# A gated-attention and maxout kernel on one core: its hand-kept order table is replaced by another

## The chip, the cores and the metric

The kernel runs on one core of one Trainium2 chip. The metric is device time in microseconds of one execution, lower is better. Before the change three executions took 138.85, 139.35 and 139.71 us (median 139.35). The profiled execution is one more, of 139.14 us; the span that its profile covers is 137.4 us.

## The reference

Four batches, eight heads, 768 time steps, head size 48. A recurrent state per head is decayed by a gate and fed with an outer product; its readout, all heads side by side, goes through a two-branch maxout layer.

```python
f = 1.0 / (1.0 + np.exp(-f_logit))
for t in range(S):                                   # S = 768
    state = f[:, :, t, :, None] * state + np.einsum('bhd,bhe->bhde', k[:, :, t], v[:, :, t])
    y[:, :, t] = np.einsum('bhd,bhde->bhe', q[:, :, t], state)
x = y.transpose(0, 2, 1, 3).reshape(B * S, H * D)    # 3072 x 384
g = np.maximum(x @ w1, x @ w2)                       # d_ff = 1024
out = g @ w_out                                      # 3072 x 384
```

## The kernel before, in words

The 3072 rows are worked in twelve stages `s = 4 * w + b`: window `w` (0 to 2) of 256 rows of batch `b` (0 to 3). A window is two chunks of 64 row pairs. Inside a stage the recurrence is done in chunked form: logs of the gate are summed by a matmul, queries and keys are scaled by exponentials of the sums, and the readout is a masked product inside the chunk plus a product with the state carried in. The maxout is rewritten with `max(a, b) = b + relu(a - b)`, so the layer is `x @ (w2 @ w_out) + relu(x @ (w1 - w2)) @ w_out`; the product `m2 = w2 @ w_out` and the difference `wd = w1 - w2` are made on the core once.

One string, `ORDER`, fixes everything: the words are read from left to right and each issues one step, so each engine gets its instructions in the order of its words. A word is a step's letter, its stage or index, an engine (`a` ScalarE, `v` VectorE, `p` GpSimd, `s` the SyncE queue; in the traces ACT, DVE, POOL, SP) and after `@` a PSUM bank (0 to 7) or, for loads, one of 30 SBUF slots. Steps that the text speaks of:

- loads, all on the one SP queue: `Lf`, `Lq`, `Lk`, `Lv` (L124, a stage's gate logits, queries, keys, values, 384 KB each), `Wb` (L140, thirds of w2), `Wo` (L144, quarters of w_out), `Wa` (L137, quarters of w1);
- on ACT: `E` (L215) and `F` (L219), the gate's exponential and logarithm; `G`, `X`, `Z` (L223, L240, L245), further exponentials;
- on DVE or POOL: `e` (L226), `i` (L249), `j` (L253, DVE only), `K` and `Q` (L260, L263, the scaled keys and queries), `V` (a cast, L113), `N` (L401);
- on TensorE (PE): `C` (L230, L233) the sums, `t`, `u` the transposes of `K` and `Q` (L278 for stages 0 and 1, L285 after), `A` (L315) the chunk product, `D` (L379) the state's increment, `S` and `y` (L336) the readout, `wt` (L463) the transposes of w2, `wm` (L478) the product m2, `d` (L418, two of the eight column blocks of `x @ wd`), `o` and `p` (L440, output products), `h` (L492, matmuls of zeros into a bank that nobody reads);
- `U` copies the transposed chunks out of PSUM (L113, tile trs), `m` masks `A` (L321, DVE), `n` adds the state (L396, L398, DVE), `Y` copies the readout (tile xT), `r` is the relu out of PSUM (L427 on ACT, L429 on DVE), `ws` makes a quarter of `wd` (L488, DVE), `b` copies an output out of PSUM;
- `z` (tile look, L113) copies one column of the readout's banks after the first half of `S`; `y` writes these banks next and so waits for it.

In stages 9 to 11 `t`, `u` and `U` are replaced by transposing DMAs (`T`, L300). `gT`, which `r` writes and `o` reads, has two buffers, for even and for odd stages. An SP transfer waits for its slot to be free, and at most eight transfers are under way, since each takes one of eight completion semaphores in turn.

Of the kernel before, what the change touches and what calls it, by code (L numbers as in the profile page):

```python
# [21 lines left out]
Lq0s@10 Lv1s@14 Z0 u1@6 K1v U1.1a@6 X0 i0p Wb0s j0v t1@5 U1.0a@5 h3@7 A1.0@3 V1a A1.1@6 D1@0 Q0p wc0a Wb1s  # L22
Wb2s m1.0@3 K0p n1.0@2 Wo1s u0@5 wt0@0 Wo3s m1.1@6 wx0v@0 S1.0@3 wc1a z1v@3 wc2p t0@2 wt1@6 n1.1@0 U0.0a@2
g0p y1 g6p U0.1v@5 wo3p wo1a S1.1@3 wt2@0 wx1v@6 Y1.0v@3 wx2v@0 A0.0@6 Lv0s@27 Y1.1a@4 Wo2s A0.1@1 wo2a V0p
wm1@3 Wo0s Lf2s@20 E2 wm3@3 Wa3s m0.1@1 m0.0@6 D0@1 wm2@3 wo0p n0.0@0 S0.0@0 z0a@0 wm0@3 F2 g3p wn2a@5 y0
# [29 lines left out]
"""


ROOMS = (1, 13, 16, 22, 28, 21, 24, 11, 21, 26, 28, 18)
M2_LAST = (0,)
WHOLE = {0, 1}  # L60
ZEROS = 29
# [3 lines left out]
def kernel(  # L65
# [491 lines left out]
```

## Time and profile before

| what | value |
|---|---|
| median of three executions | 139.35 us |
| profiled execution / its span | 139.14 us / 137.4 us |
| PE busy | 124.0 us, 90% |
| DVE / ACT / POOL busy | 96.8 / 81.0 / 52.8 us |
| DMA, read and written | 23.59 MB and 4.72 MB; the queue took 87.6% of 16 engines' span |
| first real matmul | at 6.81 us |
| last matmul ends | at about 134.45 us |

Times in rows are microseconds from the span's start. In the timeline a row is start, duration, engine, line, operation, output and inputs with shapes, how many were merged, and in brackets the idle time of that engine just before it with what ended it. PEld is the loading of a matmul's weights, which lies beside the matmuls. In the windows' rows the share of each engine is busy us in that stretch.

### The profile page before, as it was taken

How to read it: one execution, taken by the hardware profiler on the slowest of the kernel's cores; microseconds unless marked ns; L12 is line 12 of the kernel's file. 1: busy time of each engine (PE TensorE's matmuls, PEld its weight loads, DVE VectorE, ACT ScalarE, POOL GpSimd, SP SyncE). 2: the span in 40 equal slices, each digit the busy share in tenths (PEclk: the TensorE clock that was granted, in tenths of full speed). 3: DMA queues.
4: the chain of work that ended last, by engine and by line, in shares of the span. 5: the costliest groups of instructions: out<-in, count | busy, mean ns of one | idle time of the engine just before them, and what ended most of it. 6: DMA issues, size and time to landing. Idle time of an engine off the chain costs nothing.

```text
span 137.4 us, 5529 instructions
## 1 busy us (share of the span) xinstructions
PE 124.0 (90%) x2451; PEld 91.0 (66%) x2451; DVE 96.8 (70%) x153; ACT 81.0 (59%) x129; POOL 52.8 (38%) x60
## 2 busy tenths in 40 slices
PE   1058999999999999999989899999999999999991
PEld 0034796677656888665877577667878768885570
DVE  6683869497998889998898974799782786400501
ACT  3687853579869688929788967543642311252320
POOL 6006754600028643567965108699391000000000
PEclk9999999999999999999999999999999999999998
DMA  3999999999999999999999999992699400800044
GB/s 97 271 261 303 404 348 329 337 295 237 253 272 260 239 268 245 238 260 242 269 265 249 265 266 307 261 131 49 239 154 297 193 5 0 338 10 5 0 199 145
DMA packets 60904, 30.24 MB, mean 220 GB/s; under 512 B 56656, under 2 KB 58576, under 8 KB 60880
## 3 DMA queue, kind: packets, MB, share of 16 engines
q1 hardware_dynamic: 60880, 29.89, 87.6%
q8 instruction: 19, 0.31, 1.1%
q14 instruction: 5, 0.04, 0.1%
HBM read 23.59 MB, written 4.72 MB: 206 GB/s over the span
## 4 chain that ended last, share of the span: by engine, by line
PE 45%; DMA 20%; DVE 16%; SPq 7%; issue 4%; ACT 3%; POOL 1%; DVEq 0%; POOLq 0%
PE banks L440 19%; PE banks L418 14%; DMA slots<-in_q_dram 9%; SPq L124 7%; PE banks L336 7%; DMA slots<-in_moe_w_out_dram 6%; DMA slots<-in_moe_w_dram 5%; DVE at_m L321 4%; PE banks L315 2%; DVE slots L253 2%; PE banks L285 1%; DVE qp L263 1%; DVE state L401 1%; PE banks L379 1%; POOL qp L263 1%
## 5 line engine op out<-in xcount | busy, mean ns | idle before, releaser
L440 PE MATMUL banks<-wo,gT 128*128 128x384 bf16 (+1 forms) x200 | 35.3, 320 | 0.0
L418 PE MATMUL banks<-xT,wd 128*128 128x256 bf16 x288 | 34.3, 273 | 1.0 <-DVE tmp_s L396 0.5
L418 PEld LDWEIGHTS <-wd 128*128 128x128 bf16 x288 | 27.1, 98 | 5.7 <-DVE wd L488 1.2
L321 DVE TENSOR_TENSOR at_m<-banks,mask 128x1024 bf16<-128x1024 f32 x24 | 28.9, 1217 | 2.7 <-PE banks L315 2.5
L440 PEld LDWEIGHTS <-gT 128*128 128x128 bf16 x200 | 19.2, 98 | 11.8
L427 ACT ACTIVATE gT<-banks 128x1024 bf16<-128x1024 f32 (+1 forms) x17 | 16.2, 971 | 11.1 <-PE banks L418 7.1
L429 DVE TENSOR_SCALAR gT<-banks 128x1024 bf16<-128x1024 f32 (+1 forms) x9 | 9.9, 1104 | 14.8 <-PE banks L418 6.9
L263 POOL TENSOR_TENSOR qp<-slots,dec 128x768 bf16<-128x768 f32 x7 | 13.6, 1947 | 12.6 <-ACT dec L245 6.7
L113 ACT COPY slots<-banks 128x384 f32<-128x384 f32 (+1 forms) x19 | 8.8, 461 | 13.9 <-PE banks L440 13.6
L440 PE MATMUL banks<-m,xT 128*128 128x384 bf16 (+1 forms) x75 | 15.8, 320 | 0.1
L113 ACT CAST xT<-banks 128x768 bf16<-128x768 f32 (+1 forms) x12 | 8.2, 692 | 9.6 <-PE banks L336 9.6
L215 ACT ACTIVATE gate<-slots 128x768 f32<-128x768 f32 x12 | 10.1, 843 | 6.3 <-DMA slots<-in_f_logit_dram 6.3
L113 POOL CAST vb<-slots 128x768 bf16<-128x768 f32 x8 | 6.7, 840 | 15.6 <-DMA slots<-in_v_dram 15.6
L336 PE MATMUL banks<-at_m,vb 64*64 64x128 bf16 x576 | 11.4, 225 | 0.3 <-ACT look L113 0.2
L260 POOL TENSOR_TENSOR kp<-slots,inv 128x768 bf16<-128x768 f32 x6 | 10.9, 1816 | 0.6 <-ACT inv L240 0.5
L336 PEld LDWEIGHTS <-vb 64*64 64x64 bf16 x576 | 9.8, 111 | 1.6 <-issue 1.6
L253 DVE SCALAR_TENSOR_TENSOR slots<-gate,slots 128x384 f32<-128x384 f32 x12 | 9.0, 752 | 2.1 <-DMA slots<-in_q_dram 2.1
L219 ACT ACTIVATE ell<-gate 128x768 f32<-128x768 f32 x12 | 10.1, 844 | 0.3
L315 PE MATMUL banks<-trs 48*64 48x128 bf16 x384 | 10.1, 227 | 0.0
L230 PE MATMUL banks<-e,u_inc 128*128 128x384 bf16 x12 | 4.2, 355 | 6.2 <-DVE e L226 6.2
L249 POOL TENSOR_TENSOR slots<-slots,one 128x384 f32<-128x384 f32 x5 | 5.6, 1112 | 11.0 <-DMA slots<-in_k_dram 11.0
L113 DVE COPY slots<-banks 128x384 f32<-128x384 f32 (+1 forms) x9 | 5.4, 596 | 5.9 <-DMA out_dram<-slots 4.7
(69 smaller groups left out, 178.3 us busy)
## 6 DMA issues: line engine op xcount, KB each, us to landing
slots<-in_f_logit_dram SPq DMA_DIRECT2D x12, 384.0 KB, 6.2
slots<-in_q_dram SPq DMA_DIRECT2D x12, 384.0 KB, 6.0
slots<-in_k_dram SPq DMA_DIRECT2D x12, 384.0 KB, 6.3
slots<-in_v_dram SPq DMA_DIRECT2D x12, 384.0 KB, 6.1
out_dram<-slots SPq DMA_DIRECT2D x11, 384.0 KB, 3.8
slots<-in_moe_w_dram SPq DMA_DIRECT2D x3, 512.0 KB, 6.0
slots<-in_moe_w_out_dram SPq DMA_DIRECT2D x4, 384.0 KB, 8.4
slots<-in_moe_w_dram SPq DMA_DIRECT2D x4, 384.0 KB, 7.4
```

Source lines behind the costliest of these rows:

```text
L113: (nc.scalar.copy if e == "a" else engines[e].tensor_copy)(out, in_)
L215: nc.scalar.activation(flat(gate[s]), flat(loaded[s]["f"]), AF.Exp, bias=0.0, scale=-1.0)
L219: nc.scalar.activation(flat(ell[s]), flat(gate[s]), AF.Ln, bias=1.0, scale=1.0)
L253: engines[e].scalar_tensor_tensor(out=even, in0=gate[s][:, :, 1, :], scalar=1.0, in1=even, op0=ALU.add, op1=ALU.mult)
L260: engines[e].tensor_mul(pad("kp", s)[:, :, :, 0:D], by_parity(loaded[s]["k"]), both(inv[s]))
L263: engines[e].tensor_mul(pad("qp", s)[:, :, :, 0:D], by_parity(loaded[s]["q"]), both(dec[s][:, 0:HD].rearrange("p (h d) -> p h d", h=H)))
L315: nc.tensor.matmul(out=ps[h * HC:(h + 1) * HC, j % 2, par, :], lhsT=chunk(s, 0, rows, j, h)[:, par, :], rhs=chunk(s, 1, rows, j, h), start ...
L321: nc.vector.tensor_mul(at[s][:, jj].rearrange("p r j a t -> p (r j) (a t)"), banks[:, b:b + 2, :].rearrange("p r (j x) -> p (r j) x", j=2) ...
L336: nc.tensor.matmul(out=ys[s][h][c * DP:(c + 1) * DP, blk // 2, :], lhsT=lhs[:, at_col + off:at_col + off + DP], rhs=rhs, start=(s, h, c) n ...
L418: nc.tensor.matmul(out=ps[:, f, :], lhsT=wd[:, fp, kt, f * C:(f + 1) * C], rhs=xT[g][:, kt, :], start=(kt == 0), stop=(kt == KT - 1))
L427: nc.scalar.activation(dst, src, AF.Relu)
L440: nc.tensor.matmul(out=ps, lhsT=lhs, rhs=rhs[:, out_cols], start=(i == 0), stop=(i == len(terms) - 1))
```

## The change

Only the table `ORDER` and the table `ROOMS` (the slots that outputs are staged in) differ. 568 words stand in both; the two `h` words (four matmuls of zeros in all) are gone. 70 words name another engine, most of the others another bank or slot, and nearly all stand elsewhere. Counted from the PE order, the tile shape of the matmuls (128x128, 64x128 or 64x64) changes 42 times in place of 51. GpSimd gives two `K`, two `Q`, two `V` and two `e` to other engines and takes three `i` and two `N` more; VectorE has, on balance, two `e`, two `K`, two `Q` and four `V` more and three `i`, two `N`, two `r` and two copies of w2's transposes fewer.

```diff
 ORDER = """
-g2v Lf1s@7 Lf0s@23 E1 F1 E0 e1v h1@3 g4p Lq1s@17 C1@7 F0 j1v Z1 e0v Q1v Lk1s@26 G1 C0@2 X1 i1v g7v G0 Lk0s@3
+Lf1s@11 E1 Lf0s@10 Lq1s@21 g2p F1 E0 Lk1s@24 e1v Wb1s Lv1s@25 g3v g0p F0 e0v j1v G0 C1@1 X1 Lk0s@3 Wb2s Z1
...
-ROOMS = (1, 13, 16, 22, 28, 21, 24, 11, 21, 26, 28, 18)
+ROOMS = (13, 20, 25, 26, 11, 16, 21, 0, 15, 25, 11, 2)
```

The SP queue, from the first load of values on, before. `in_moe_w_dram 128x1024` is w2 and `128x3x256` is w1; the `in_f_logit_dram` row is the gate of stage 2.

```order
L124 DMA slots<-in_v_dram 128x8x96
L140 DMA slots<-in_moe_w_dram 128x1024 x3
L144 DMA slots<-in_moe_w_out_dram 128x768 x2
L124 DMA slots<-in_v_dram 128x8x96
L144 DMA slots<-in_moe_w_out_dram 128x768 x2
L124 DMA slots<-in_f_logit_dram 128x8x96
L137 DMA slots<-in_moe_w_dram 128x3x256 x3
```

The same queue after, up to the same two weights.

```order
L124 DMA slots<-in_q_dram 128x8x96
L140 DMA slots<-in_moe_w_dram 128x1024
L137 DMA slots<-in_moe_w_dram 128x3x256 x2
L124 DMA slots<-in_v_dram 128x8x96
L144 DMA slots<-in_moe_w_out_dram 128x768 x3
L124 DMA slots<-in_f_logit_dram 128x8x96
L144 DMA slots<-in_moe_w_out_dram 128x768
```

Two quarters of w1 moved ahead of all of w_out, and one quarter of w_out behind the gate of stage 2, so that this gate is the 17th transfer where it was the 16th.

ACT around the gate of stage 2 (`gate_147`) and the look of stage 0, before:

```order
L113 CAST xT_403<-banks 128x6x64
L113 CAST wo<-slots 128x768
L215 ACTIVATE gate_147<-slots 128x768
L113 COPY look<-banks 128x1
L219 ACTIVATE ell_158<-gate_147 128x768
```

And after (`gate_148` is the gate of stage 2, `gT_481` the relu of stage 1):

```order
L113 COPY slots<-banks 128x8x128
L427 ACTIVATE gT_481<-banks 128x1024
L113 CAST wo<-slots 128x768
L215 ACTIVATE gate_148<-slots 128x768
L113 COPY look<-banks 128x1
L219 ACTIVATE ell_156<-gate_148 128x768
```

A relu of stage 1 now stands ahead; the look stays behind the gate's exponential in both.

PE at the program's start, as a piece of the difference (L492 are the matmuls of zeros):

```order
 L552 UNCONDITIONAL_BRANCH
-L492 LDWEIGHTS slots
-L492 MATMUL banks<-slots 128x512
 L230 LDWEIGHTS u_inc
 L230 MATMUL banks<-e_97,u_inc 128x384
```

The zeros ahead of the first sums are gone; so are the three that stood ahead of the first `A`.

More of the change, by code (lines that the diff above doesn't have):

```diff
@@ L20 @@
 ORDER = """
-g2v Lf1s@7 Lf0s@23 E1 F1 E0 e1v h1@3 g4p Lq1s@17 C1@7 F0 j1v Z1 e0v Q1v Lk1s@26 G1 C0@2 X1 i1v g7v G0 Lk0s@3
[L22 to L25, printed above, removed]
@@ new lines @@
+n1.0@2 wt1@5 wt2@0 S1.0@6 wc0a j0v g6v m1.1@2 K0p z1v@6 Q0p Wa2s ws2v wx1a@5 y1 S1.1@6 Wa3s u0@4 n1.1@2
+wx2v@0 ws3v Y1.0a@6 wt0@3 Lv0s@8 Wo1s Wo3s Wo2s Y1.1a@7 t0@7 d1.2@5 wo1p wo2p V0v U0.0v@7 d1.3@6 U0.1a@4
+wx0a@3 Lf2s@26 D0@1 A0.0@3 n0.0@0 S0.0@6 Wo0s wo0p n0.1@1 r1.1a@5 m0.0@3 wo3a E2 A0.1@5 wm1@0 m0.1@5 Lf3s@24
+Wa0s z0a@6 wm3@0 F2 e2v y0 S0.1@6 wm2@0 Y0.0v@6 G2 C2@3 Y0.1a@7 Wa1s E3 wm0@0 Lq3s@8 F3 Lq2s@2 ws0v e3v ws1v
+wn1a@1 wn2a@2 d0.2@4 d0.3@5 C3@2 Lk2s@22 j3v Z2 r0.1a@4 Lk3s@15 wn0v@0 Z3 N1.1p d0.0@6 Q3v d0.1@7 r0.0a@6
@@ new lines @@
+i7p m5.1@2 d4.2@0 Lq11s@15 r4.0a@6 G8 U6.2v@4 Q7p S5.0@6 r4.1a@0 z5v@6 A6.0@4 y5 m6.0@4 K7p E9 i8p D6@2
+A6.1@0 S5.1@6 n6.0@0 Lf10s@27 Y5.2a@6 o4.1@5 d5.3@2 m6.1@0 d5.0@0 Lv8s@12 V7a F9 N6.0v Lq9s@16 b4.1.0a@5 j8v
+d5.2@1 r5.1a@1 e9v S6.0@4 z6v@4 D7@6 S6.1@4 y6 n7.0@0 E10 Lv10s@17 C9@6 d5.1@1 Y6.2v@4 V8a r5.0a@0 Z9
+Lk10s@22 Lv9s@6 j9v Lk9s@28 o4.0@2 K8v Q8p X9 n6.1@2 F10 d6.3@1 N7.0p d6.2@0 b4.0.0v@2 n7.1@0 N5.1p G10
+Lf11s@2 d6.1@5 G9 Q9p d6.0@4 r6.1a@0 r6.0a@4 u7@2 t7@2 t8@6 U7.2v@2 u8@6 o5.1@0 Lq10s@12 V10v D8@1 U8.2a@6
@@ new lines @@
+A10.0@6 Tk11s D11@5 n10.0@1 A11.0@2 Y9.2a@0 n11.0@2 O0.2s A11.1@0 m11.0@2 N10.0v O2.2s d9.1@5 d9.0@4 d9.3@3
+m10.0@6 d9.2@2 m11.1@0 o7.0@6 O5.2s r9.0v@4 o8.0@7 N11.0p b7.0.0a@6 r9.1a@2 A10.1@0 S11.0@4 z11a@4 O3.2s
+S10.0@2 y11 m10.1@0 S11.1@4 O6.2s z10v@2 y10 S10.1@2 Y10.2a@2 Y11.0v@4 O7.2s b8.0.0v@7 o8.1@0 O4.2s
+b8.1.0a@0 Y11.1v@5 d10.1@4 d10.0@3 O8.2s r10.0v@3 O1.2s d10.2@6 d11.0@1 d10.3@7 d11.1@0 d11.2@5 d11.3@4
+o9.1@2 r10.1v@6 o9.0@7 r11.5a@4 b9.0.0a@7 o10.1@3 o10.0@7 r11.2v@1 r11.4v@5 b10.1.0v@3 r11.3a@0 b9.1.0a@2
@@ L54 @@
+p11.1.1@0 b10.0.0a@7 O10.2s O9.2s o11.0@2 p11.1.0@5 b11.1.2a@0 b11.0.0v@2 O11.0s b11.1.1a@5 O11.1.2s
 O11.1.1s
 """
[L58 removed]
+ROOMS = (13, 20, 25, 26, 11, 16, 21, 0, 15, 25, 11, 2)
 M2_LAST = (0,)
```

44 lines of the change are left out of this document (16 added, 28 removed).

## The prediction

> **What bounds the kernel now.** I read the busy times of the page first, then the windows, which cut the span at the places where the work changes.
>
> ```profile
> span 137.4 us, 5529 instructions
> PE 124.0 (90%) x2451; PEld 91.0 (66%) x2451; DVE 96.8 (70%) x153; ACT 81.0 (59%) x129; POOL 52.8 (38%) x60
> ```
>
> ```profile
> 12.00:20.40 8.40, 8.36 (x153) 6.30 (x153) 5.47 (x9) 5.83 (x6) 5.56 (x5) 1.00 1.08 368
> 20.40:40.00 19.60, 19.01 (x321) 12.98 (x310) 16.31 (x24) 13.27 (x23) 3.85 (x6) 1.00 1.10 290
> 40.00:60.00 20.00, 19.61 (x482) 14.68 (x480) 18.11 (x22) 16.27 (x29) 11.89 (x13) 1.00 1.10 254
> 60.00:80.00 20.00, 18.95 (x459) 13.93 (x451) 17.23 (x27) 15.97 (x23) 11.27 (x11) 1.00 1.13 257
> 80.00:95.00 15.00, 14.97 (x338) 10.80 (x338) 12.34 (x17) 8.05 (x16) 10.86 (x8) 1.00 1.06 211
> 95.00:112.00 17.00, 16.82 (x416) 12.88 (x409) 11.83 (x18) 7.26 (x10) 6.05 (x6) 1.00 0.72 181
> 112.00:134.45 22.45, 22.44 (x292) 16.86 (x289) 7.53 (x10) 6.07 (x12) 0.00 (x0) 1.00 0.24 93
> 134.45:137.40 2.95, 0.00 (x0) 0.00 (x0) 0.00 (x0) 0.32 (x1) 0.00 (x0) 0.85 0.31 109
> ```
>
> Columns are the stretch, its length, then busy us of PE, weight loads, DVE, ACT, POOL, the granted clock, the DMA share and GB/s. PE is the bound from 12 us to 134.45 us. Between 40 and 112 us it idles 0.39 + 1.05 + 0.03 + 0.18 = 1.65 us in all, so no order can win more than that there by removing idle time alone. DVE, 18.11 of 20 us at most, is the runner-up between 40 and 80 us. The queue is full (share above 1) until 95 us, but PE hardly waits for it after 40 us. From 112 us on PE is closed, and 2.95 us of copy and store follow. So the time is PE's start, its work, and its stalls. The opening decides the start:
>
> ```profile
> 6.81 0.48 PE L230 MATMUL banks<-e,u_inc 128*128 128x384 bf16 x1 [5.02 <-DVE e L226]
> 11.78 1.49 PE L492 MATMUL banks<-slots 128*128 128x512 bf16 x3
> 13.20 1.07 PE L315 MATMUL banks<-trs 48*64 48x128 bf16 x32
> 18.14 1.06 PE L463 MATMUL banks<-ident,slots 128*128 128x128 bf16 x8
> 19.13 1.47 PE L336 MATMUL banks<-at_m,vb 64*64 64x128 bf16 x48
> 20.70 0.62 PE L463 MATMUL banks<-ident,slots 128*128 128x128 bf16 x8
> 21.82 2.12 PE L478 MATMUL banks<-wo,slots 128*128 128x384 bf16 x12
> 26.69 0.89 PE L336 MATMUL banks<-at_m,vb 64*64 64x128 bf16 x48
> 34.36 0.65 PE L440 MATMUL banks<-m,xT 128*128 128x384 bf16 x3
> ```
>
> The same eight transposes take 1.06 us at 18.14 and 0.62 us at 20.70, the same 48 matmuls 1.47 and 0.89 us: up to about 20 us PE runs at about 0.6 of its later speed, though the windows' clock column says 1.00 there. The matmul group at 26.69 is `y0`, the one at 34.36 the first output product.
>
> **The opening, +0.8 us.** In before `y0` starts right after a chain from the queue:
>
> ```profile
> 25.68 0.84 ACT L215 ACTIVATE gate<-slots 128x768 f32<-128x768 f32 x1 [1.67 <-DMA slots<-in_f_logit_dram]
> 26.43 0.14 ACT L113 COPY look<-banks 128x1 f32<-128x1 f32 x1
> 23.18 0.83 ACT L113 CAST wo<-slots 128x768 bf16<-128x768 f32 x1 [1.90 <-DMA slots<-in_moe_w_out_dram]
> 24.26 0.83 POOL L113 CAST wo<-slots 128x768 bf16<-128x768 f32 x1 [1.23 <-DMA slots<-in_moe_w_out_dram]
> 26.84 0.96 DVE L488 TENSOR_TENSOR wd<-slots 128x768 bf16<-128x768 f32 x1 [1.65 <-DMA slots<-in_moe_w_dram]
> ```
>
> ACT waits for the gate of stage 2, exponentiates it, then does the look `z0a`, and `y0` follows. Each of these rows starts when its transfer lands, so differences of starts are transfer times: a quarter of w_out 24.26 - 23.18 = 1.08 us, a quarter of w1 26.84 - 25.68 = 1.16 us. The new queue puts two quarters of w1 ahead of this gate and takes one of w_out away: 2 x 1.16 - 1.08 = +1.24 us, a landing at 26.92, and `y0` at 27.93. ACT's order keeps the look behind the exponential. What is late next would be the second mask, on DVE; I take it as no later than the look.
>
> From `y0` to the first output product before takes 34.36 - 26.69 = 7.67 us. After, two of the eight `d` stand ahead of `y0` and two `wm` behind it. A `d` costs 6.72 / 10 = 0.67 us, a `wm` 2.12 / 2 = 1.06:
>
> ```profile
> 116.96 6.72 PE L418 MATMUL banks<-xT,wd 128*128 128x256 bf16 x60
> PEld L418 <- DVE wd L488: 1.2, 3, 0.6
> ```
>
> The three waits for `wd` (1.2 us) should go, since half of w1 lands earlier and PE comes to the rest later. So 7.67 - 1.34 + 2.12 - 1.2 = 7.25 us, the first output product at 35.18, +0.8 us. Bounds: 0, if PE is not yet through with what stands ahead of `y0`, so that the wait is covered; +2.0, if the waits for `wd` stay.
>
> **Fewer changes of shape, -0.8 us.**
>
> ```profile
> 109.12 0.66 PE L440 MATMUL banks<-m,xT 128*128 128x384 bf16 x3
> 111.01 0.42 PE L315 MATMUL banks<-trs 48*64 48x128 bf16 x16
> 112.42 0.65 PE L440 MATMUL banks<-m,xT 128*128 128x384 bf16 x3
> 114.21 0.82 PE L418 MATMUL banks<-xT,wd 128*128 128x256 bf16 x6
> ```
>
> An output product followed by another shape takes 111.01 - 109.12 = 1.89 us, one followed by its own shape 114.21 - 112.42 = 1.79. A change costs 0.1 us; nine fewer are -0.9, and I take -0.8, since one or so lies beside a wait. Bounds 0 and -0.9.
>
> **Waits in the middle, -0.8 us.** The longest is this:
>
> ```profile
> 73.69 2.41 POOL L263 TENSOR_TENSOR qp<-slots,dec 128x768 bf16<-128x768 f32 x1 [1.55 <-DMA slots<-in_q_dram]
> 74.93 1.58 DVE L226 TENSOR_TENSOR e<-ell 128x384 bf16<-128x384 f32 x1 [0.51 <-ACT ell L219]
> 76.84 0.81 PE L418 MATMUL banks<-xT,wd 128*128 128x256 bf16 x6 [0.54 <-DVE tmp_s L396]
> ```
>
> A `d` of stage 5 needs the bank that `n6.1` reads, and that stands behind a slow `e` on DVE. After, it takes bank 1 and this wait goes. But the new order has its own: `A6.0` behind `U6.2` on DVE, `u4` behind three multiplications there. Of the 1.65 us I let half go. Bounds: -1.65 (all gone) and +1.0 (as much again, by the length of the waits that stand now).
>
> **A copy handed to ACT, +0.3 us.** `U8.2` moves from DVE to ACT behind `r6.0`:
>
> ```profile
> L113 ACT COPY trs<-banks 128x2048 bf16<-128x2048 bf16 x1 | 1.9, 1865 | 0.3 <-PE banks L285 0.3
> L113 DVE COPY trs<-banks 128x2048 bf16<-128x2048 bf16 x5 | 6.0, 1215 | 1.6 <-PE banks L285 1.6
> ```
>
> `A7.0` needs one of the banks that it reads. PE has the transposes and an output product in between (about 3 us), ACT a relu of 1.0 and the copy of 1.87: just covered if ACT starts at once. I take +0.3, between 0 and +0.9.
>
> **Work on DVE, +0.2 us.** Ten `e`, `K`, `Q`, `V` come to DVE and nine `i`, `N`, `r` and copies of w2 go, each between 0.35 and 1.2 us; the balance is about +2 us. Against it:
>
> ```profile
> 58.97 1.81 POOL L260 TENSOR_TENSOR kp<-slots,inv 128x768 bf16<-128x768 f32 x1
> 59.17 2.03 DVE L253 SCALAR_TENSOR_TENSOR slots<-gate,slots 128x384 f32<-128x384 f32 x1 [0.27 <-DMA slots<-in_q_dram]
> 73.00 0.55 DVE L253 SCALAR_TENSOR_TENSOR slots<-gate,slots 128x384 f32<-128x384 f32 x1
> L253 DVE SCALAR_TENSOR_TENSOR slots<-gate,slots 128x384 f32<-128x384 f32 x12 | 9.0, 752 | 2.1 <-DMA slots<-in_q_dram 2.1
> ```
>
> The same step takes 0.55 us alone and 2.03 beside a `K` on POOL; over the twelve that is 9.0 - 12 x 0.55 = 2.4 us of DVE's time. POOL's `K` and `Q` fall from 13 to 9, so some 0.7 us of this comes back, and more on `e` and `N`. I take +0.2 on the path, between -0.5 and +1.8. The Trainium skill (SBUF — State Buffer, Who interferes with whom) has this as an exclusive lock: a DVE instruction with two SBUF inputs blocks while a GpSimd instruction that reads SBUF holds the shared ports. The rows of 59.17 and 74.93 agree; by that rule every `K` or `Q` taken off POOL frees DVE, this term would be -0.4 and the sum 0.6 us lower.
>
> Output copies, slots and the last 17 us keep their kind and length: there the chain is ten `d` and seven products in both, and the last store the same. I cost them at nothing; the closed PE hides them.
>
> **The sum.** +0.8 - 0.8 - 0.8 + 0.3 + 0.2 = -0.3 us. The profiled execution took 139.14 us (1.74 around its span), so 138.84; the median of the three lies 0.21 above it, which gives 139.05, said as 139.0.
>
> **Rivals.** *The opening's debt is repaid.* From 40 to 60 us DVE paces PE (18.11 of 20 us), and a PE that arrives late there finds its masks and keys ready. Then the +0.8 is gone at 60 us and the middle's 1.65 us go whole: -0.8 - 1.65 + 0.3 + 0.2 = -1.95, 137.4 us. For it speaks that PE idles in this stretch at all; against it, that 19.61 of 20 us leaves little to repay with. Chance 0.25.
>
> *DVE becomes the bound, slower.* If its +2 us falls whole into 40 to 80 us, where it has 4.66 us free in total, and the idle time between its waits cannot be used, PE waits where it now idles: +1.8 instead of +0.2, and the middle's waits stay, +0.8. That is +2.4 on the forecast, 141.4 us. It decides once DVE is busy for over 19 of the 20 us from 40 to 60. Chance 0.13.
>
> *The clock comes later.* The zeros before 13.20 kept PE at work; without them it has holes before the first `A` (whose queries now come from POOL) and before `y1`. From 13.20 to about 20.4 us PE worked 7.2 us without a long hole before it sped up. If it must start again at `y1`, about 18.8, the slow time lasts to 26.0, 5.6 us longer, and loses 5.6 x (1 - 0.62 / 1.06) = 2.3 us; the wait before `y0` covers some 0.9 of it. That is +1.4, 140.4 us; it is over 1% from 27 us on. Chance 0.12. The Trainium skill (TensorE: Matmul & The Clock Gate, Part 1) lets the clock up after one window of about 3.4 us of sustained work. By that rule the rows of 18.14 and 19.13 would already be fast; they are not, and the trace decides. The same page (Part 4) says that transposes do not count as busy in the same way; many of the rows in question are transposes, which would fit, but no run here shows it.
>
> That the table doesn't do what it says is no rival: the 42 changes can be counted and half of w1 stands where it is said to.
>
> **Chances.** Forecast 0.48, the rivals 0.25, 0.13 and 0.12, anything else 0.02. About 1%, 1.4 us, is what a measurement of this kernel can tell from no change. Faster by more than that (under 137.96): most of the first rival and a tenth of the forecast, 0.26. Slower (over 140.74): most of the second, some of the third and a little of the forecast, 0.18. Within: 0.56. The range 137.2 to 141.0 leaves out the lower half of the first rival and most of the upper part of the second; the forecast's own range is 138.0 to 140.2.
>
> **What the profile after would show.** Opening: ACT's gate of stage 2 starts at about 26.9 after a wait for DMA, `y0` near 27.9, the first L440 near 35.2; `y0` by 27.0 would refute the term. Clock: a group of eight L463 or L278 between 20.5 and 23 takes 0.6 us; 1.0 would be the third rival. Shapes: PE busy falls by some 2 us, of which 1.49 are the zeros of 11.78. Middle: PE's idle time from 40 to 112 is about 0.8 us. Copy: a wait of PE or its weight loads for ACT trs near 85 us. DVE: L253's mean falls from 752 ns; 19 or more of 20 us busy from 40 to 60 would be the second rival. A last matmul at another distance than about 2.95 us from the end, or a load that PE waits for after 40 us, would show a mistake that I have not priced.

## The result: 0.8% slower

The changed kernel takes 140.7 us (median), the one before 139.5 us in the same runs; the ratio is 1.0084, 95% interval 1.0063 to 1.0105. That is +1.2 us where I had said -0.3. It lies inside the range and inside "within 1%", but the sign is wrong and the difference is larger than its error. Ratios here and below are taken over the executions within 1.5% of the fastest one of their kernel, at least eight of twelve where twelve were made. The profiled execution took 140.88 us, its span is 139.0 us.

The page's busy line and the windows of the changed kernel, cut at the same places (columns as in the prediction):

```profile
PE 121.1 (87%) x2447; PEld 91.0 (65%) x2447; DVE 96.7 (70%) x154; ACT 83.1 (60%) x130; POOL 47.2 (34%) x58
```

```profile
12.00:20.40 8.40, 6.77 (x150) 5.63 (x148) 6.57 (x12) 5.53 (x7) 4.63 (x3) 1.00 1.11 332
20.40:40.00 19.60, 18.62 (x273) 13.68 (x271) 14.63 (x22) 15.21 (x25) 3.72 (x5) 1.00 1.03 283
40.00:60.00 20.00, 18.84 (x475) 14.16 (x467) 17.54 (x22) 16.06 (x28) 9.45 (x12) 1.00 0.99 235
60.00:80.00 20.00, 19.59 (x572) 14.99 (x571) 15.83 (x25) 15.29 (x24) 16.38 (x15) 1.00 1.09 249
80.00:95.00 15.00, 15.00 (x230) 10.10 (x227) 11.53 (x18) 10.83 (x17) 5.57 (x6) 1.00 1.01 194
95.00:112.00 17.00, 16.66 (x442) 13.94 (x442) 13.47 (x20) 7.74 (x11) 3.03 (x3) 1.00 1.01 216
112.00:136.10 24.10, 23.62 (x315) 16.94 (x313) 9.21 (x13) 5.79 (x12) 0.00 (x0) 1.00 0.26 102
136.10:139.00 2.90, 0.00 (x0) 0.00 (x0) 0.00 (x0) 0.00 (x0) 0.00 (x0) 0.90 0.39 136
```

PE is busy 2.9 us less, yet the end is later: PE idles more, above all ahead of 60 us. From 40 to 112 us it idles 1.16 + 0.41 + 0.00 + 0.34 = 1.91 us (before 1.65). Behind 112 us it is as good as closed: the last matmul ends at 135.72, so 0.38 of the 0.48 us that the window shows lie behind it. The queue's share from 20 to 60 us has fallen from 1.10 to about 1.0.

**The opening**, in the timeline:

```profile
9.23 1.80 POOL L263 TENSOR_TENSOR qp<-slots,dec 128x768 bf16<-128x768 f32 x1 [5.83 <-ACT dec L245]
9.59 1.86 DVE L249 TENSOR_TENSOR slots<-slots,one 128x384 f32<-128x384 f32 x1 [0.70 <-ACT one L223]
14.63 1.07 PE L315 MATMUL banks<-trs 48*64 48x128 bf16 x32 [1.10 <-ACT trs L113]
20.58 1.03 PE L278 MATMUL banks<-ident,qp 128*128 128x128 bf16 x8
22.25 0.66 PE L278 MATMUL banks<-ident,kp 128*128 128x128 bf16 x8
25.68 2.12 PE L478 MATMUL banks<-wo,slots 128*128 128x384 bf16 x12
26.72 0.85 ACT L215 ACTIVATE gate<-slots 128x768 f32<-128x768 f32 x1 [0.72 <-DMA slots<-in_f_logit_dram]
27.48 0.14 ACT L113 COPY look<-banks 128x1 f32<-128x1 f32 x1
27.78 0.89 PE L336 MATMUL banks<-at_m,vb 64*64 64x128 bf16 x48
```

The gate of stage 2 starts at 26.72 and `y0` at 27.78, as forecast (26.92, 27.93). But PE had not waited for it here: its first two `wm` end at 27.80. PE itself is late, since `Q1` went to POOL and, beside it, DVE's step on the keys of stage 1 takes 1.86 us, and since it still runs slowly at 20.58 (1.03 us for the eight transposes). In the timeline of before:

```profile
9.28 0.55 DVE L249 TENSOR_TENSOR slots<-slots,one 128x384 f32<-128x384 f32 x1
```

So the first `A` starts at 14.63 instead of 13.20. Two causes cover each other at `y0`, and I had seen one. Which of them ends last differs between executions: in the profiles of late_end and slots (told below), with the same order up to there, PE comes up to speed earlier, does the first matmul of `y0` at 26.78 and 26.33, and then waits for the look, 0.78 and 0.93 us, as the prediction had it.

**Behind it**, a wait that I had not listed, and the queue on the chain of waits (second fence: start, length, what):

```profile
34.37 0.56 DVE L253 SCALAR_TENSOR_TENSOR slots<-gate,slots 128x384 f32<-128x384 f32 x1 [1.59 <-DMA slots<-in_q_dram]
34.84 0.55 DVE L113 CAST m<-banks 128x384 bf16<-128x384 f32 x1
35.45 0.81 PE L418 MATMUL banks<-xT,wd 128*128 128x256 bf16 x6 [0.75 <-DVE m L113]
36.10 1.46 PE L440 MATMUL banks<-wo,gT 128*128 128x384 bf16 x8
45.60 0.82 POOL L113 CAST vb<-slots 128x768 bf16<-128x768 f32 x1 [2.19 <-DMA slots<-in_v_dram]
46.48 0.44 PE L379 MATMUL banks<-vb,kp 64*64 64x48 bf16 x32 [0.57 <-POOL vb L113]
```

```profile
33.83 5.89 DMA slots<-in_f_logit_dram
39.74 0.85 ACT gate L215
40.62 4.93 DMA slots<-in_v_dram
```

`d1.0` needs the bank that a copy of m2 reads, and that copy stands on DVE behind a query that has not landed. And the load of the value of stage 2 goes into slot 25, where the gate of stage 5 lies: SP issues it only at 40.62, after ACT has read the gate (39.74 + 0.85); it lands at 45.5 and `D2` waits.

**The tail.** Before `y9`, and the last five stores of the queue in the kernel before and in the changed one:

```profile
106.13 0.16 DVE L113 COPY look<-banks 128x2 f32<-128x2 f32 x1 [1.22 <-PE banks L336]
106.34 0.86 PE L336 MATMUL banks<-at_m,vb 64*64 64x128 bf16 x46 [0.34 <-DVE look L113]
```

```profile
131.38 3.77 SPq L453 DMA_DIRECT2D out_dram<-slots  x5
```

```profile
132.66 4.08 SPq L453 DMA_DIRECT2D out_dram<-slots  x5
```

A `y` follows its `S` through a look on DVE or ACT. In the order before, other steps stood between `S9.0` and `y9`; grouped by shape, nothing stands there. The five stores take 0.31 us longer, since `O11.0`, whose copy comes late, now stands ahead of a store that is ready; the last matmul ends 3.28 us before the end instead of 2.96.

**Where the lag arises.** To compare places in orders that differ, I give each step of PE one length (an output product 1.79 us, a `d` 0.655, and so on from the rows; changes of shape aren't counted) and ask when each trace had done the same sum. The row of `y0` goes by its second matmul, since the first can run ahead of the look. Lag of several kernels behind the one before, us (the runs are told below; late_end and splice_c have the changed kernel's order up to 100 us):

| at | changed | late_end | splice_c | q1_on_dve | gate_earlier | slots | splice_slots_c |
|---|---|---|---|---|---|---|---|
| first A | 1.43 | 1.41 | 1.48 | -0.12 | 1.40 | 1.54 | 1.49 |
| y0 | 1.81 | 1.79 | 1.52 | 1.67 | 2.51 | 1.49 | 1.94 |
| C4, 47 to 49 us | 2.34 | 0.68 | 1.04 | 1.07 | 1.13 | 0.41 | 0.71 |
| A4.0, 59 to 61 us | 1.83 | 0.22 | 0.82 | 1.03 | 0.64 | -0.08 | 0.22 |
| y8, 98 to 100 us | 0.64 | 0.18 | 1.17 | 0.62 | -0.02 | -0.05 | -0.64 |
| last matmul | 1.28 | 0.80 | 1.92 | 1.27 | 0.63 | 0.60 | 0.38 |

Two things can be read. The first three columns have one order up to `y8` and differ there by 1 us, so a single profile places a loss in the middle only to about that; there the timed ratios decide. And in the five columns that don't end with the old order the lag grows from `y8` to the last matmul by 0.62 to 0.65 us, each time (late_end, whose tail was edited, too). With the 0.31 us of the last stores, which late_end doesn't have, that is 1.0 us which the changed tail costs in these profiles.

### The profile page after: what moved, and what is told of

It is laid out like the page before. It is cut to its first block, busy times and chain, and to the rows that moved or that the text cites. A ratio compares the mean times of both kernels' runs of the same rounds, so it can differ in the third digit from the quotient of the medians.

```text
span 139.0 us, 5507 instructions
## 1 busy us (share of the span) xinstructions
PE 121.1 (87%) x2447; PEld 91.0 (65%) x2447; DVE 96.7 (70%) x154; ACT 83.1 (60%) x130; POOL 47.2 (34%) x58
## 4 chain that ended last, share of the span: by engine, by line
PE 73%; DMA 10%; DVE 6%; ACT 6%; issue 1%; POOL 1%; SPq 0%; DVEq 0%
PE banks L440 26%; PE banks L418 21%; PE banks L336 10%; DMA slots<-in_f_logit_dram 7%; PE banks L315 4%; DMA slots<-in_v_dram 4%; PE banks L478 3%; DVE at_m L321 2%; PE banks L285 2%; PE banks L379 2%; PE banks L278 2%; ACT gate L215 2%; PE banks L230 1%; DVE slots L249 1%; ACT ell L219 1%
## 5 line engine op out<-in xcount | busy, mean ns | idle before, releaser
L427 ACT ACTIVATE gT<-banks 128x1024 bf16<-128x1024 f32 (+1 forms) x19 | 18.5, 979 | 16.2 <-PE banks L440 8.3
L113 ACT COPY slots<-banks 128x384 f32<-128x384 f32 (+2 forms) x22 | 11.1, 513 | 14.4 <-PE banks L440 14.3
L401 POOL TENSOR_TENSOR state<-tmp_s,dec 128x192 bf16<-128x192 f32 x12 | 8.3, 695 | 16.9 <-DVE tmp_s L396 16.8
L263 POOL TENSOR_TENSOR qp<-slots,dec 128x768 bf16<-128x768 f32 x5 | 9.5, 1899 | 10.0 <-ACT dec L245 8.0
L429 DVE TENSOR_SCALAR gT<-banks 128x1024 bf16<-128x1024 f32 (+1 forms) x7 | 7.4, 1070 | 7.3 <-PE banks L440 3.7
L249 POOL TENSOR_TENSOR slots<-slots,one 128x384 f32<-128x384 f32 x8 | 8.0, 1004 | 9.6 <-DMA slots<-in_k_dram 6.3
L113 POOL CAST vb<-slots 128x768 bf16<-128x768 f32 x6 | 5.0, 825 | 17.5 <-PE banks L285 11.2
L113 ACT CAST xT<-banks 128x768 bf16<-128x768 f32 (+1 forms) x10 | 6.9, 699 | 5.6 <-PE banks L336 5.5
L113 ACT COPY trs<-banks 128x1024 bf16<-128x1024 bf16 (+1 forms) x5 | 6.7, 1348 | 4.1 <-PE banks L278 4.1
L315 PEld LDWEIGHTS <-trs 48*64 48x64 bf16 x384 | 7.1, 111 | 3.1 <-issue 1.6
```

Source lines behind the costliest of these rows:

```text
L113: (nc.scalar.copy if e == "a" else engines[e].tensor_copy)(out, in_)
L249: engines[e].tensor_mul(even, even, one[s])
L263: engines[e].tensor_mul(pad("qp", s)[:, :, :, 0:D], by_parity(loaded[s]["q"]), both(dec[s][:, 0:HD].rearrange("p (h d) -> p h d", h=H)))
L315: nc.tensor.matmul(out=ps[h * HC:(h + 1) * HC, j % 2, par, :], lhsT=chunk(s, 0, rows, j, h)[:, par, :], rhs=chunk(s, 1, rows, j, h), start ...
L401: engines[e].tensor_mul(heads_of(state_of(s)[:, h]), tmps.pop((s, h)), decay(s, h))
L427: nc.scalar.activation(dst, src, AF.Relu)
```

## The experiments

All edits are words of the order. Ratios are to the kernel before, measured beside it; a difference in us is that of two ratios, of 139.5 us, with both errors. Theory: queue, tail and opening each take a part. Rivals: the landing of the gate of stage 2 alone (my term); the clock; the queue alone. In the first four runs the program is one line shorter, so the profile's line numbers are one lower there.

**1. The opening.** `q1_on_dve`: `Q1` back on DVE, with ACT's order for it.

```
-F0 e0v j1v G0 C1@1 X1 Lk0s@3 Wb2s Z1 G1 C0@5 i1v K1v Lq0s@23 Q1p u1@7
+F0 j1v C1@1 Z1 Lk0s@3 Wb2s G1 e0v Q1v X1 G0 C0@5 i1v K1v Lq0s@23 u1@7
```

> The changed kernel with the queries of stage 1 multiplied on DVE again and ACT in the order that feeds them (all else as changed). Theory, two causes that cover each other: the first A comes at 13.1 to 13.4 us instead of 14.63, the clock is up about 1.3 us earlier, but y0 still waits for the gate of stage 2 (landing 26.7), so it starts at 27.5 to 27.8 and the time falls by 0.3 us at most, ratio to before 1.006 to 1.009. Rival, POOL's multiplication alone: y0 at 26.7 or earlier and 1.2 us gained, ratio 1.000. Rival, the queue paces the stages behind: the same time as changed, whatever y0 does, 1.008.

Measured: 1.0113 (1.0081 to 1.0145), 0.4 ± 0.5 us more than changed. The first `A` comes 1.55 us earlier, and `y0` where theory had it: its first matmul runs at 27.12, the other 47 wait 0.32 us for the look behind the gate and start at 27.65. The time did not fall at all, so it fits the second rival (the same as changed) best. At 61 us this profile is 0.8 us ahead of the changed one; at `C9`, at 79.5 in both, the lag is back at 1.35 us. The gate of stage 9 lands at 73.5 in both, and PE, which is earlier here, waits for a look that stands on DVE behind the sum made from it:

```profile
73.46 0.84 ACT L214 ACTIVATE gate<-slots 128x768 f32<-128x768 f32 x1 [1.08 <-DMA slots<-in_f_logit_dram]
```

```profile
78.48 0.36 PE L335 MATMUL banks<-trs,state 48*64 48x128 bf16 x12 [0.59 <-DVE look L112]
```

The sum itself is why: here, and then in the changed kernel,

```profile
76.13 1.81 POOL L262 TENSOR_TENSOR qp<-slots,dec 128x768 bf16<-128x768 f32 x1 [0.77 <-DVE slots L252]
76.50 1.86 DVE L225 TENSOR_TENSOR e<-ell 128x384 bf16<-128x384 f32 x1 [0.44 <-ACT ell L218]
```

```profile
76.61 0.56 DVE L226 TENSOR_TENSOR e<-ell 128x384 bf16<-128x384 f32 x1
76.63 2.22 POOL L263 TENSOR_TENSOR qp<-slots,dec 128x768 bf16<-128x768 f32 x1 [0.76 <-DVE slots L253]
```

POOL is earlier with PE, the gate is not, so POOL's `Q` now starts before DVE's sum, and the sum takes 1.86 us in place of 0.56. The lead is lost there; section 2 has the same again.

`gate_earlier`: the gate ahead of the third quarter of w_out.

```
-Wo1s Wo3s Wo2s ... Lf2s@26
+Wo1s Wo3s Lf2s@26 Wo2s
```

> The changed kernel with the load of the gate of stage 2 one transfer earlier, ahead of the third quarter of w_out. The prediction's term (the landing alone sets y0): y0 at 26.7, first L440 1.1 us earlier, 1.0 us gained, ratio 1.001. Theory, two causes that cover each other: ACT exponentiates the gate at 25.6, but PE is not through with the third wm before 27.8, so y0 stays at 27.7 and the ratio at 1.007 to 1.009.

Measured: 1.0042 (1.0008 to 1.0075), 0.59 ± 0.55 us less than changed (by the medians of all executions 0.2). In its profile `y0` is later, not earlier (28.49), because PE's clock came later there (below). So the edit may be worth something; whether it is, and by which way, stays open.

`q1_and_gate`: both.

> Both edits together. Theory, two causes that cover each other: y0 at 26.5 to 26.8, 1.0 to 1.2 us earlier than changed; of this 0.5 to 1.2 us reach the end, ratio 0.9995 to 1.005. Rival, the queue paces the stages behind (the query of stage 3 lands at 34.37, the keys of stage 3 at 40.72): the lag is back at the transposes of stage 3 at 40.7, and the ratio stays at 1.007 to 1.009.

Measured: 1.0079 (1.0040 to 1.0117), 0.1 ± 0.6 us less than changed, although `y0` is at 26.82, 1.0 us earlier. A start that is 1 us earlier is not seen at the end. The ratio is the rival's, its place isn't: the transposes of stage 3 start at 39.63, 1.1 us ahead of the changed profile (40.77), and the lead is gone only at `C9` (79.31 against 79.49). That the queue takes it back is not shown.

**2. The queue.** `slots`: four loads go where nobody is in the way.

```
-Lv0s@8 ... Lq3s@8 ... Lv2s@25 ... Lk4s@25
+Lv0s@16 ... Lq3s@17 ... Lv2s@28 ... Lk4s@19
```

> The changed kernel with four loads in other, free slots (value of stage 0 in 16, query of stage 3 in 17, value of stage 2 in 28, key of stage 4 in 19), so that the queue does not wait for a slot. Theory, the queue's waits cost 0.6 us: the waits of SP before the quarter of w_out at 22.9, the query of stage 3, the value of stage 2 and the key of stage 4 are gone, the query of stage 3 lands 1 us or more before 34.37, D2 does not wait for POOL's vb, and 0.4 to 0.9 us are gained, ratio 1.002 to 1.006. Rival, the opening alone: PE comes to d1.0 and t3 no earlier, so 0 to 0.2 us, ratio 1.007 to 1.009.

Measured: 1.0020 (0.9989 to 1.0051), 0.9 ± 0.5 us less than changed. SP issues the value of stage 2 at 37.38 instead of 40.62 (40.00 in late_end, with the changed kernel's slots), and the wait of `D2` is gone. The time is as expected. That C4 starts 1.9 us earlier shows little: in late_end and gate_earlier, whose slots are as changed, it is 1.7 and 1.2 us earlier as well.

`slots2`: two more, that stood 2.5 us each.

```
-Lf6s@23 ... Lk8s@24
+Lf6s@21 ... Lk8s@1
```

> As the run with four loads in other slots, and two more: the gate of stage 6 in slot 21 and the key of stage 8 in slot 1, whose loads stood 2.5 and 2.6 us at the queue until a value and a key had been read out. Theory, the queue paces: the gate of stage 9 lands 2 us or more before 72.6, the sum e of stage 9 is no longer 2.0 us long beside POOL's multiplication, PE's wait before S6.1 at 77.8 (0.9 us) goes, and 0.5 to 0.8 us more are gained: ratio 0.996 to 0.999. Rival, those two stops are hidden by loads that come early enough: 0 to 0.2 us, 1.001 to 1.003.

Measured: 1.0094 (1.0058 to 1.0131), 1.0 ± 0.7 us *more* than with four. Expected was 0.5 to 0.8 us less. The two stops are gone, the loads land earlier, and this is what follows at 52 us, first with four, then with six:

```profile
51.74 0.55 DVE L252 SCALAR_TENSOR_TENSOR slots<-gate,slots 128x384 f32<-128x384 f32 x1
52.04 1.11 POOL L248 TENSOR_TENSOR slots<-slots,one 128x384 f32<-128x384 f32 x1 [2.43 <-DMA slots<-in_k_dram]
```

```profile
51.37 1.50 POOL L249 TENSOR_TENSOR slots<-slots,one 128x384 f32<-128x384 f32 x1 [1.92 <-DMA slots<-in_k_dram]
51.92 1.36 DVE L253 SCALAR_TENSOR_TENSOR slots<-gate,slots 128x384 f32<-128x384 f32 x1
54.47 0.82 PE L418 MATMUL banks<-xT,wd 128*128 128x256 bf16 x6 [0.48 <-DVE gT L429]
```

The key of stage 5 lands 0.7 us earlier, POOL starts on it before DVE's step instead of during it, DVE's step takes 1.36 us instead of 0.55, the relu behind it is 1 us late, and PE waits. Earlier loads are not a gain by themselves; here they moved POOL's work beside DVE's. The wait seen is 0.48 us; where the other half of the 1.0 us arises was not followed.

`slots2_q1`: the six with `Q1` on DVE.

> The six loads in other slots and the queries of stage 1 on DVE, with ACT's order for them. Theory, a queue that doesn't stop lets the opening count: 0.5 to 1.0 us less than with the six slots alone, ratio 0.990 to 0.995. Rival, the start is not carried to the end even then (the lag is gone at the transposes of stage 3): within 0.3 us of the six slots alone.

Measured: 1.0022 (0.9985 to 1.0059), 1.0 ± 0.7 us less than the six alone, and as the four. The difference is the expected one, the ratio isn't (0.990 to 0.995). By the runs above the start should not do that; why it does here was not followed.

`all2`: the six slots, the two edits of late_end, and the copy of m2 ahead of the query (`-j3v ... wn0v`, `+wn0v j3v`).

> The six loads in other slots, the two late edits, and the copy of m2 on DVE ahead of the query of stage 3. Theory, queue and late waits add up: 1.2 to 1.7 us less than the changed kernel and 0.2 to 0.6 us less than before, ratio 0.993 to 0.999, and the wait of PE for DVE's m at 35.45 is gone. Rival, the late waits are repaid elsewhere: no better than the six slots alone.

Measured: 1.0035 (1.0003 to 1.0067). The wait of `d1.0` is gone; the wait for the relu at 54 us is there again (0.47 us). It is 0.8 ± 0.7 us less than the six slots alone, but not faster than before, as had been expected.

**3. The tail.** By now the runs of sections 1 and 2 with four slots had shown the same lag growing behind 100 us, and the theory became that the tail makes most of the loss. The expectations count it from `A9.0` on (0.93 us, with 0.35 for the stores 1.28); from `y8`, where the kernel before has no wait of its own in between, it is 0.65 and 0.31.

`late_end`: fillers between `S9.0` and `y9`, and the ready store first.

```
-m9.0@2 z9v@0 r8.0a@6 y9 S9.1@0 V11v D10@3 Tq10s A10.0@6 Tk11s D11@5
+V11v m9.0@2 z9v@0 r8.0a@6 D10@3 D11@5 y9 S9.1@0 Tq10s A10.0@6 Tk11s
-O11.0s b11.1.1a@5 O11.1.2s O11.1.1s
+O11.1.2s O11.0s b11.1.1a@5 O11.1.1s
```

> The changed kernel with two edits behind 100 us: the state products D10 and D11 stand between S9.0 and y9 again (with the copy of the value of stage 11 ahead of the mask of stage 9, where DVE has nothing to do), and the store O11.1.2 ahead of O11.0. Theory, the lag of the changed kernel is made in the last third, where a closed PE keeps whatever is lost: the wait of 0.34 us (0.53 in all) before y9 falls to 0.1 or less, the last matmul lies 2.9 to 3.0 us before the end instead of 3.28, and 0.6 to 0.9 us are gained: ratio 1.002 to 1.005. Rival, the queue and the opening make the whole loss: 0 to 0.2 us, 1.007 to 1.009.

Measured: 1.0039 (1.0013 to 1.0064), 0.6 ± 0.5 us less than changed, the expected time, but half by luck. The stores are right: five in 3.77 us, the last matmul 2.86 us before the end.

```profile
132.18 3.77 SPq L453 DMA_DIRECT2D out_dram<-slots  x5
```

But the fillers gain nothing: the wait before `y9` is gone, and another of the same size stands behind it.

```profile
107.83 0.42 PE L315 MATMUL banks<-trs 48*64 48x128 bf16 x16 [0.44 <-ACT xT L113]
```

`A11.1` takes the bank that the copy of `y9` reads on ACT. The same two products can cover either the look or the copy, not both; the order before had an output product for the second.

`splice_rev`: the order before up to `o7.1` (101 us), the changed order from there (`A9.0@2`, `A9.1@6`, D10 left to the second part).

> The reverse: the order of the kernel before up to stage 7's second output product, then the changed kernel's order to the end. Theory, the loss is made behind 100 us: 1.0 to 1.4 us slower than before, ratio 1.007 to 1.010, with the wait for a look ahead of y9 and the last matmul 3.28 us before the end. Rival, opening and queue make it: within 0.3 us of before, ratio 0.998 to 1.002.

Measured: 1.0138 (1.0101 to 1.0174), 1.9 ± 0.5 us slower than before. The wait of 0.34 us before `y9` is there, the lag grows by 0.65 us from `y8` to the last matmul, as in the others, and the stores cost 0.33. The rest, 0.8 us, stands between 94 and 100 us, where the two orders meet: waits of 0.39 us at `D9` and 0.34 us at `y8`. The sum, 1.8 us, fits what was timed; the joint's share of it is known from this one profile.

The other way round, the changed order up to `o7.1`, the order before from there, with D10 between:

```
+... C11@2 d7.0@6 d7.1@7 ... d7.3@3 d7.2@2 ... A9.0@6 i11v A9.1@4 D10@3 n10.0@2 N9.0p N10.0p
+o7.1@2 Y8.2a@0 O0.2s O6.2s O5.2s m9.0@6 d8.1@7 m9.1@4 K11p Tk10s ... (as before)
```

> The changed kernel's order up to stage 7's second output product (about 101 us), then the order of the kernel before, from that product to the last store; in the piece between them the banks of A9, D10 and four d are chosen so that the two fit. Theory, the loss is made behind 100 us (0.93 us of waits between 104 and 117 us, 0.35 us at the last stores) and the start is repaid by then: 1.1 to 1.3 us less than the changed kernel, ratio 0.998 to 1.001, with the last matmul 2.95 us before the end. Rival, opening and queue make it: still 1.005 to 1.009.

> The same, with the four loads in other slots in its first part. Theory, the loss is made behind 100 us and the queue adds some: 0.3 to 0.7 us less than the same order without them, ratio 0.993 to 0.998, faster than before. Rival, the queue's stops are covered: the same as without them, within 0.2 us.

Measured: 1.0168 (1.0126 to 1.0210), and with the four slots 1.0121 (1.0058 to 1.0183). In these two, Z11 and X11 stand behind the `d` that takes their bank, so the keys and queries of stage 11 are made from other numbers, and both wait for that `d`. They say nothing about the tail. `splice_b` puts Z11 and X11 ahead of it; `splice_slots_zeros` adds the four slots and the zeros of section 4:

> The changed kernel's order up to stage 7's second output product, then the order of the kernel before, now with the exponentials of stage 11 (X11, Z11) read ahead of the d that takes their bank. Theory, the tail's waits and its last stores cost 1.28 us: ratio 0.998 to 1.002, the last matmul 2.95 us before the end. Rival, the tail is repaid or lost elsewhere: 1.005 to 1.009.

> The mended splice, with the four loads in other slots and the four matmuls on zeros. Theory, tail, queue and zeros add up: 0.3 to 1.0 us faster than before, ratio 0.993 to 0.998. Rival, they cover each other: not faster than the mended splice, 0.998 to 1.002.

Measured: 1.0156 (1.0101 to 1.0210), and 1.0024 (0.9986 to 1.0063). The profiled execution of the first had a granted clock of 0.75 from 40 us on, so its places aren't read. That of the second shows what the joint costs:

```profile
109.72 0.42 PE L315 MATMUL banks<-trs 48*64 48x128 bf16 x16 [1.57 <-DMA trs<-kp]
```

The key of stage 11 is transposed by the queue, behind three stores. `splice_c` puts that right:

```
-i11v A9.1@4 ... O0.2s O6.2s O5.2s ... K11p Tk10s ... Tq10s ... Tq11s ... Tk11s
+i11v K11p A9.1@4 ... Tq10s Tq11s Tk10s Tk11s O0.2s O6.2s O5.2s
```

> The mended splice (the changed kernel's order up to stage 7's second output product, then the order of the kernel before) with the key of stage 11 multiplied first on POOL and the four transposes by DMA ahead of three output stores, so that PE no longer waits 1.57 us for that key. Theory, the changed kernel's tail costs 1.28 us: ratio 0.998 to 1.002. Rival, start, queue and PE's instruction stream cost it: 1.005 to 1.009.

> The same with the four loads in other slots. Theory, tail and queue add up: 0.4 to 0.9 us less than the run without them, ratio 0.992 to 0.997, faster than before. Rival, they cover each other: within 0.2 us of the run without them.

Measured: 1.0060 (1.0028 to 1.0092), 0.3 ± 0.5 us less than changed where 1.1 to 1.3 was expected, so in the rival's range; with the four slots 0.9937 (0.9897 to 0.9977), 1.7 ± 0.7 us less than that and faster than the kernel before. The last is less sure than its interval says: the twelve executions spread from 138.0 to 141.8 us, and by the medians of all of them the gain of the slots is 0.85 us and the lead on the kernel before 0.15. In both profiles the waits before `y9`, `A11.1` and `y11` are gone and the last matmul ends 2.9 us before the end. Against that stands one new hole in each, 1.0 and 1.2 us from one matmul to the next, within a step of PE that waits for no other engine; here in the one with slots:

```profile
111.80 0.41 PE L315 MATMUL banks<-trs 48*64 48x128 bf16 x13 [1.01 <-issue]
```

It is one of PE's own stops (last section). So the tail's 1.0 us is shown in the profiles, and the time of the reverse splice agrees; that taking it away saves 1.0 us is not shown, since what replaced it had a loss of its own. The four slots were timed twice and gained both times, with about the same size by the medians (0.8 and 0.85 us).

**4. The zeros.** The kernel before without its four matmuls on zeros; with all four ahead of `C1`; and the changed kernel with them at their old places:

```
-h1@3 ... h3@7        (before_nozeros)
-h1@3 ... h3@7  +h4@3 (before_zeros_early)
+h1@3 C1@1 ... h3@3 A1.0@6  (zeros)
```

> The kernel before without its four matmuls on zeros (which the output doesn't need). The prediction's clock rival: the fast clock comes 1.9 us or more later, y0 comes 0.5 to 1 us later and the time is 0.5 to 1.5 us longer, ratio 1.004 to 1.010. Theory, the start is repaid before 100 us, and the clock's time differs between executions anyway: ratio 0.998 to 1.002.

> The kernel before with all four matmuls on zeros ahead of C1, where PE waits for nothing but the first gate, and none ahead of the first A. If the zeros act by the clock at the first A: as slow as without them, ratio 1.004 to 1.009. If they act by the number of instructions, that is by the place at which PE's instruction stream stops: ratio 0.998 to 1.002.

> The changed kernel with the four matmuls on zeros of the kernel before: one ahead of C1, three ahead of the first A. Theory, the start is not carried to the end: ratio 1.006 to 1.010 as without them. Rival, the zeros are worth in the changed kernel what they are worth in the one before: 0.6 to 1.0 us less, ratio 1.001 to 1.004.

Measured: 1.0067 (1.0043 to 1.0092); 0.9996 (0.9967 to 1.0024); 1.0076 (1.0037 to 1.0114). The kernel before needs its zeros, by 0.9 us, but not where they stood, and the changed kernel gains nothing from them. In the kernel before it isn't the clock: without zeros the eight transposes at 20.56 take 0.62 us, as those at 20.70 before, and up to 48 us that profile runs level with before. Then this:

```profile
48.74 0.46 PE L336 MATMUL banks<-at_m,vb 64*64 64x128 bf16 x15
50.49 0.65 PE L336 MATMUL banks<-at_m,vb 64*64 64x128 bf16 x31 [1.29 <-issue]
```

PE stops for 1.3 us in the middle of the 48 matmuls of `y2`, none of which waits for another engine. The clock as the cause falls, above all by the second run: zeros that stand far ahead of the first `A` serve as well. The place of PE's stops as the cause fits these three runs; it isn't proved by them, since each has one profile.

In the changed kernel the zeros do move the clock. The first transposes of w2, with zeros and without:

```profile
16.09 0.62 PE L463 MATMUL banks<-ident,slots 128*128 128x128 bf16 x8
```

```profile
16.06 2.05 PE L463 MATMUL banks<-ident,slots 128*128 128x128 bf16 x16
```

Eight take 0.62 us where sixteen take 2.05. The time doesn't follow (0.1 ± 0.6 us less): an earlier clock, too, is not seen at the end.

## Why the prediction was wrong

*The sum*, -0.3 us: measured +1.2. The step that failed is the one that cost nothing: "Output copies, slots and the last 17 us ... I cost them at nothing; the closed PE hides them." The slots cost 0.9 ± 0.5 us in time, the tail 1.0 us in the profiles. The prediction had named two signs of such a mistake, another distance of the last matmul from the end and a load that PE waits for after 40 us, and both came: 3.28 us, and the value of stage 2 at 46.48. The terms, in its order:

*Opening, +0.8.* The landing came as worked out (26.72), and so did `y0`. In the changed profile that was luck: "what would be late next ... no later than the look" failed, since PE's own work came last, by `Q1` on POOL and the slow clock; in late_end and slots it held. The three waits for `wd` did go, but 7.25 us became 36.10 - 27.78 = 8.32, since the wait for the copy of m2 (0.75 us by its row) took their place. In late_end, with the same order, it is not there; it hangs on when a query lands. And the step "+0.8 at the first output product, so +0.8 at the end" was wrong in kind: q1_and_gate moved `y0` by 1.0 us, and the end moved by 0.1 ± 0.6.

*Shapes, -0.8.* PE's busy time fell by 2.9 us, 1.49 of it the zeros; the rest leaves room for the 0.8. It was not measured alone. Six of the nine fewer changes lie ahead of `y0` (7 for 13), where a gain doesn't reach the end; between `A4.0` and `y8` there are even three more (18 for 15). So the fall of the lag from 1.83 us at 61 to 0.64 at 100 us isn't this gain, and it isn't the order's: late_end and slots, with the same steps there, lag as much at 100 us as at 60. The repayment of the first rival is not shown by it.

*Middle waits, -0.8.* Wrong: 1.91 us of idle time, not 0.8. Of it 0.57 us stand at `D2`, by the queue, and 0.34 before `y9`, which is the tail's. I had called the queue full and not looked into it for loads that wait for a slot. That was worth 0.9 ± 0.5 and 1.7 ± 0.7 us, and it stood in the table: slots 8 and 25 take three loads each within 41 us.

*The copy on ACT, +0.3.* Nothing: `A7.0` follows `D8` at once.

```profile
87.86 0.37 PE L379 MATMUL banks<-vb,kp 64*64 64x48 bf16 x12
88.04 0.25 PE L315 MATMUL banks<-trs 48*64 48x128 bf16 x2
```

*DVE, +0.2.* DVE is busy 17.54 of 20 us from 40 to 60, so the second rival is out, and L253 takes its bare time again:

```profile
L253 DVE SCALAR_TENSOR_TENSOR slots<-gate,slots 128x384 f32<-128x384 f32 x12 | 6.5, 550 | 1.8 <-DMA slots<-in_q_dram 1.8
```

550 ns where it was 752: the port came free as the rule of the Trainium skill (SBUF — State Buffer, Who interferes with whom) has it. The same rule at the start took 1.3 us back (1.86 for 0.55 at 9.59), where `Q1` had been put on POOL; I had counted `K` and `Q` as a number, not by place.

*Output copies, slots, the last 17 us, nothing.* Wrong in all three: slots as above, the tail 0.65 us, the stores 0.31. "The closed PE hides them" had the logic upside down: where PE is closed, every new wait on it reaches the end.

*Third rival, the clock.* Its sign came true (1.03 at 20.58, 0.66 at 22.25), and its cause in part: with the zeros back the clock is up at 16.09. Its price did not: the zeros gave the changed kernel 0.1 ± 0.6 us, not 1.4.

## What to carry to other kernels

A gain or loss counts where nothing behind it can absorb it: price the last stretch, where the bound engine is closed, first and step by step, and the opening last. Follow every load to the step that empties its slot; the loads behind it on the same queue wait with it. And when a wait is removed, look at what then runs side by side: an earlier load made a slower DVE.

## What the runs showed of the hardware

**The clock rises at a time that differs.** Three kernels whose first work on PE is the changed kernel's (gate_earlier, slots, splice_c), the same kind of eight transposes:

```profile
22.23 1.06 PE L277 MATMUL banks<-ident,kp 128*128 128x128 bf16 x8
```

```profile
19.81 0.62 PE L277 MATMUL banks<-ident,qp 128*128 128x128 bf16 x8
```

```profile
20.37 0.62 PE L278 MATMUL banks<-ident,qp 128*128 128x128 bf16 x8
```

gate_earlier is still slow at 22.23, the changed kernel at 20.58; slots and splice_c are fast by 19.81 and 20.37. With the same work from 14.6 us on, the clock turns before 19.8 us in one execution and after 23.2 in another; over the nine profiles with this opening (five of them with loads in other slots) `y0` starts, by its second matmul, between 27.47 and 28.52, so a single profile carries 1 us of chance there. With zeros ahead of the first `A` the transposes at 16 us are fast in both profiles that have them (zeros and splice_slots_zeros); without them they are slow in all profiles with this opening. My rule, about 7.2 us after the first `A` without a long hole, doesn't hold. The Trainium skill (TensorE: Matmul & The Clock Gate, Part 1) gives one window of about 3.4 us of sustained work; slots, fast by 19.81, leaves room for that; gate_earlier, at work from 14.6 us and still slow at 22.23, doesn't agree.

**PE stops at fixed places of its program, for its instructions.** Counting PE's matmuls from the start, the holes inside a step that waits for nothing lie at numbers 223, 607, 735, 1119, 1247, 1375, and 2141 or 2142, over nineteen profiles: the distances are multiples of 128 (the last within two). A hole takes 0.3 to 1.5 us, and which of the places show one differs between executions; 1119 shows one in ten profiles, among them the changed kernel's. Taking four matmuls out moves every later step by four places against this grid. "issue" is all that the waits show, but the page of the profile also lists the DMA of the instructions (here of the changed kernel), and the packed trace has the time of each packet:

```profile
q8 instruction: 19, 0.31, 0.9%
```

Nineteen packets of 16 KB in each profile, one for each 128 pairs of weight load and matmul or so (2447 / 19 = 129). Every one of the 22 holes ends 1.27 to 1.60 us after one of these packets has landed, and each 128 matmuls further the packet is the next one. In before_nozeros it lands at 48.96 and PE goes on at 50.49; in the kernel before it lands at 47.47, and the same place passes at 48.93 without a hole. In splice_c and splice_slots_c it lands at 111.97 and 110.34, and PE goes on at 113.33 and 111.80. So a hole is a wait for instructions that come late; why a packet comes earlier in one execution than in another was not followed.
